# One attention and feed-forward kernel: the first batch's q and k rows laid nine to a partition, and the order of the work drawn up anew

## The chip, the core and the metric

The kernel runs on one core of a Trainium2 chip. The metric is the device time of one execution in microseconds (us), median of several runs. Beside it stands one profiled execution, from which every row below is read.

## The reference

The inputs q, k and v have 8 batches, 8 heads, 576 rows and 64 columns. Two attentions are added, and their sum goes through a gated feed-forward layer:

```python
S, D, factor = 576, 64, 4
q_d = q.reshape(B, H, S // 4, 4, D).mean(axis=3)       # k_d and v_d alike
out_d = softmax(scale * q_d @ k_d.T) @ v_d              # 144 x 144 scores
out_up = np.repeat(out_d, 4, axis=2)
mask = np.abs(pos[:, None] - pos[None, :]) < 4
out_local = softmax(np.where(mask, scale * q @ k.T, -1e9)) @ v
x = (out_up + out_local).transpose(0, 2, 1, 3).reshape(4608, 512)
h = x @ w_in                                            # 512 -> 2048
g = h * np.clip(h + 3.0, 0.0, 6.0) / 6.0
out = g @ w_out                                         # 2048 -> 512
```

## The kernel before

A batch has 8 heads, taken in pairs; a pair of one batch is a **unit**, so batch 0 has the units U0 to U3, and a head of a unit fills 64 of the 128 partitions. For each unit q and k are needed turned, with the 64 columns on the partitions. Then come the pooled attention (sums of four rows in `pool4`, L428 to L434; scores L528; softmax; product with v L711) and the banded one (scores L740 in tiles of 64 columns under a mask that L732 adds; row maxima L584, subtraction L587, exponential L590 and L595, scaling L610 and L612; turning L765; product with v L783). L788 adds the two into `first`, the rows of x for that unit.

The feed-forward part is computed with every operand split into a rounded part (hi, a CAST on L128 for ACT or L130 for DVE) and the remainder (lo, L972), three matmuls for one product. The weights are split as well, in pieces `rawp0`, `rawp1`, ...: for one piece ACT does L195 and L208, DVE does L210 and L200, then a CAST makes hi and L220 makes lo. GEMM1 is L1064 (h = x w_in), then relu on ACT L1070, gate on DVE L1074, splits, and GEMM2 L1114. Four units are the four quarters of the contracted dimension of GEMM1: its matmuls with the quarter of U3 can start only when U3's `first` is split, and before that only 18 matmuls (those of U0 to U2 for two tiles of h) stand ahead of them on PE.

Everything is recorded first as a list of operations. A planner then gives each operation a due time and places them one after the other on the engines, by estimated costs (`COST`), by penalties that steer an operation to one of the engines that can do it (`PEN`, by kind of work: "lo" is L220, "xlo" L972, "ev" the copies out of PSUM, "norm" and "normd" L612, L610), and by an offset of each unit's due time (`SHIFT`, one number for a unit, 32 in all). The outcome is a fixed order of instructions on every engine; the times in the planner do not exist on the chip, which only waits for semaphores.

In batch 0 alone q and k are turned by PE. `plan_first` loads rows as they lie in memory; `turn_rows` (L404) turns 128 rows in one matmul with the identity; `evict_rows` copies the result out of PSUM (L128 on ACT, L130 on DVE) so that row p * 4 + r lands where row number p * 4 + r belongs. In the kernel before, a partition holds four consecutive rows, which covers 512 of the 576; `half` and `main` load these, and `last` loads the 64 rows left over, k's on one half of the partitions and q's on the other. So k's 512 rows, q's 512 rows and both leftovers are turned by separate groups of matmuls (4, 4 and 1), and k's turned rows need only k's load and the leftovers.

The DMAs of U0 and of the leftovers are issued by ACT and SP in turn, everything else by SP: nine issues for q and k stand on SP ahead of the first for v. Batch 1 and later load q and k turned by DMA and DVE, and the diff leaves them alone. Dummy matmuls (L1498) fill PE while it has nothing to do in the first 30 us.

Of the kernel before, what the change touches and what calls it, by code (L numbers as in the profile page):

```python
# [17 lines left out]
B, H, S, D = 8, 8, 576, 64  # L18
DM, DFF = 512, 2048
P = 128  # L20
# [11 lines left out]
ROW = 2 * D  # L32
# [24 lines left out]
def tile_local_down_attention_moe(ctx, tc, q_all, k_all, v_all, _qk_loc, _v_loc, w_in, w_out, ident_d, _mask_d, out):  # L57
# [188 lines left out]
    def src(t, first, ap):  # L246
        return bass.AP(tensor=t.tensor, offset=t.offset + first * ROW, ap=ap)
# [3 lines left out]
    def plan_first():  # L251

        def duo(d):
            if ("rows", d) not in begun:
                begun["rows", d] = buf("rawd", (0, d), [P, 2, 9, ROW])
            return begun["rows", d]

        def row0(d):
            return 2 * d * NC * RP

        def main(i, d, u, n, eng):
            t = (q_all, k_all)[i]
            if n == 1:
                eng.dma_start(duo(d)[:, u, 4 * i:4 * i + 4], src(t, row0(d) + u * S, [[4 * ROW, P], [1, 4 * ROW]]))
            else:
                eng.dma_start(
                    duo(d)[:, :, 4 * i:4 * i + 4], src(t, row0(d), [[4 * ROW, P], [S * ROW, 2], [1, 4 * ROW]]))

        def half(i, d, h, eng):
            eng.dma_start(  # L270
                duo(d)[D * h:D * h + D, 0, 4 * i:4 * i + 4],
                src((q_all, k_all)[i], row0(d) + 4 * D * h, [[4 * ROW, D], [1, 4 * ROW]]))

        def last(i, d, eng):
            eng.dma_start(
                duo(d)[i * D:(i + 1) * D, :, 8], src((q_all, k_all)[i], row0(d) + 4 * P, [[ROW, D], [S * ROW, 2], [1, ROW]]))

        def begin(eng, what, *args, size):
            o = op(eng, 0.5, partial(what, *args, {"ACT": nc.scalar, "SP": nc.sync}[eng]),
                   take=[("rawd", (0, args[1]))], size=size, dl=-1.0)  # L280
            loads.append(o)
            return o

        for d in range(2):
            for u in range(2 - d):
                for i in (1, 0):
                    n = 1 + d
                    if u + d == 0:
                        os = [begin(eng, half, i, d, h, size=dma(D, 2048)) for h, eng in enumerate(("ACT", "SP"))]
                    else:  # L290
                        os = [begin("SP", main, i, d, u, n, size=dma(n * P, 2048))]
                    for x in range(u, u + n):
                        begun["main", d, x, i] = os
                if u == 0:
                    for i in (1, 0):
                        begun["last", d, i] = begin("ACT" if i and not d else "SP", last, i, d, size=dma(2 * D, 512))

        def sums_rest():
            begun["raw rest"] = t = buf("raw4r", 0, [4 * KR, NHP, ROW])
            nc.sync.dma_start(t, src(v_all, 4 * P, [[ROW, 4 * KR], [S * ROW, NHP], [1, ROW]]))  # L300

        def raw(d):
            begun["raw", d] = t = buf("raw4", (0, d), [P, 2, 4, ROW])
            nc.sync.dma_start(t, src(v_all, row0(d), [[4 * ROW, P], [S * ROW, 2], [1, 4 * ROW]]))

        def sum_rest():
            begun["ps rest"] = ps = bank("s", ("v4", 0))
            nc.tensor.matmul(
                ps[:KR, :NHP * ROW], four[:4 * KR, :KR], begun["raw rest"].rearrange("p n e -> p (n e)"), start=True, stop=True)

        def evict_rest(eng):
            begun["rest"] = t = buf("vr0", 0, [KR, NHP, ROW])
            copy_on(eng, t.rearrange("p n e -> p (n e)"), begun["ps rest"][:KR, :NHP * ROW])

        l = op("SP", 0.5, sums_rest, take=[("raw4r", 0)], size=dma(4 * KR * NHP, 512))
        loads.append(l)
        for d in range(2):
            begun["v", d] = o = op("SP", 0.5, partial(raw, d), take=[("raw4", (0, d))], size=dma(2 * P, 2048))
            loads.append(o)
        key = "s", ("v4", 0)  # L320
        a = op("PE", 0.95, sum_rest, [l, masked[1]], take=[key], free=[("raw4r", 0)], lag=LAGT, rec=2)
        begun["vr"] = op(on("ev", NHP * ROW), 0, evict_rest, [a], take=[("vr0", 0)], free=[key])
        early_users.extend([a, begun["vr"]])
# [49 lines left out]
    def plan_unit(b, d, u, row0, k0, kv, PS, masked, early_user, due):  # L373
# [32 lines left out]
        def evict_rows(i, eng):  # L406
            if "qk" not in st:
                st["qk"] = buf("qkd" + k0, un, [P, 2, S])
            if i < 2:
                copy_on(eng, st["qk"][:, i, :4 * P].rearrange("e (p r) -> e p r", r=4),  # L410
                        st["psq", i].rearrange("e (r p) -> e p r", r=4))
            else:
                copy_on(eng, st["qk"][:, :, 4 * P:], st["psq", i][:, :P].rearrange("e (i p) -> e i p", i=2))

        if b < BY_PE:
            rk, evs = ("rawd", (0, d)), {}
            for i in (1, 0, 2):
                key = PS, ("qk", un, i)
                lds = begun["main", d, u, i] if i < 2 else [begun["last", d, x] for x in range(2)]
                a = early_user(op("PE", 0.17 if i == 2 else 0.5, partial(turn_rows, i), lds + masked[:1],  # L420
                                  take=[key, ("qkd" + k0, un)], free=[rk], lag=LAGT, rec=1 if i == 2 else 4))
                evs[i] = op(on("ev", P if i == 2 else 4 * P), 0, partial(evict_rows, i), [a], free=[key])
# [13 lines left out]
        for kind, t in (("q", q_all), ("k", k_all)):  # L436
            hk = kind, un
            if b < BY_PE:
                a = turned[kind] = [evs["qk".index(kind)], evs[2]]
            else:  # L440
                l = op("SP", 2.0, partial(ldt, t, kind), loads if b == 1 else [], take=[("qk", hk)], size=dma(4 * S, 128), nd=4)
                a = turned[kind] = [op("DVE", 0.72, partial(turn, kind), [l])]
            pooled[kind] = early_user(op(
                on("pool4", 1.0), 0, partial(pool4, kind), a, take=[("p4" + k0, hk)]))
# [1131 lines left out]
PAIR0 = 6  # L1576

SHIFT = [
# [32 lines left out]
    "ob": {"ACT": (0.6, 0.0), "DVE": (0.64, 0.0)},  # L1611
}
PEN = {
    "lo": {"DVE": -73.8},
    "low": {"DVE": -9.2},
    "whi": {"DVE": -43.5},
    "ghi": {"DVE": -19.7},
    "pool4": {"POOL": 106.6},
    "ev": {"DVE": 130.1},
    "sum4": {"POOL": 26.0},  # L1620
    "norm": {"DVE": -42.6},
    "normd": {"DVE": 29.2, "ACT": 7.3},
    "minus": {"DVE": 27.2},
    "xhi": {"DVE": 47.9},
    "xlo": {"POOL": -152.3},
    "gl": {"POOL": -18.1},
    "ob": {"DVE": 37.5},
}


# [471 lines left out]
```

## Time and profile before

| | us |
|---|---|
| median of 3 runs | 896.82 |
| their range | 896.68 to 896.88 |
| profiled execution: its own time | 893.89 |
| profiled execution: span from first to last instruction | 892.1 |
| PE busy | 884.6 (99%) |
| DVE busy | 620.9 (70%) |
| ACT busy | 420.9 (47%) |
| POOL busy | 204.2 (23%) |

The profiled execution took 1.79 us beside its span, and 2.93 us less than the median of the runs that were timed without a profile. Busy times are of the whole span; the share of one stretch can be very different, and the first 35 us are.

### The profile page before, as it was taken

The page shows a single profiled execution, that of the slowest core. Times are in us where ns is not written, and L with a number is a line of the kernel's source. Part 1 is how long each engine was busy: PE and PEld are TensorE (multiplying, and loading weights), DVE is VectorE, ACT ScalarE, POOL GpSimd, SP SyncE. Part 2 cuts the span into 40 slices and gives each one's busy share as a digit, 9 for nine tenths or more (in the row PEclk, how much of TensorE's full clock was granted, in tenths as well). Part 3 has the DMA queues.
Part 4 walks back from the last instruction along what each step waited for, and adds up shares of the span by engine and source line. Part 5 has one row for each costly group of instructions (what it writes and reads, how often), then busy time and mean ns, then how long its engine had stood idle before and what let it go on. Part 6 is the DMA issues. An engine that isn't in the chain of part 4 may idle for free.

```text
span 892.1 us, 19653 instructions
## 1 busy us (share of the span) xinstructions
PE 884.6 (99%) x7060; PEld 720.5 (81%) x7060; DVE 620.9 (70%) x1182; ACT 420.9 (47%) x1432; POOL 204.2 (23%) x278
## 2 busy tenths in 40 slices
PE   8999999999999999999999999999999999999997
PEld 5777778888888888888888888888888888888886
DVE  7998886766854676667755784667666689876541
ACT  6967754544662456344532563445444154434200
POOL 5543533311422041313230130114122000000000
PEclk9999999999999999999999999999999999999999
DMA  9996643654664456635654567555642221222431
GB/s 249 303 262 196 149 121 98 118 113 100 121 148 92 92 118 142 133 60 104 135 121 80 117 125 213 110 109 112 148 97 62 53 71 48 77 66 71 144 93 49
DMA packets 316209, 107.47 MB, mean 120 GB/s; under 512 B 249552, under 2 KB 295632, under 8 KB 316112
## 3 DMA queue, kind: packets, MB, share of 16 engines
q1 hardware_dynamic: 315494, 105.44, 49.8%
q8 instruction: 56, 0.92, 0.4%
q10 hardware_dynamic: 618, 0.77, 0.3%
q14 instruction: 41, 0.34, 0.1%
HBM read 77.25 MB, written 28.90 MB: 119 GB/s over the span
## 4 chain that ended last, share of the span: by engine, by line
PE 98%; ACT 1%; DMA 0%; ACTq 0%; issue 0%
PE o L1114 35%; PE h L1064 34%; PE o L1329 5%; PE a L1265 5%; PE h L1265 4%; PE a L1329 2%; PE h L1329 2%; PE a L740 2%; PE h L783 2%; PE a L545 1%; PE h L690 1%; PE o L1064 1%; PE a L528 0%; DMA arena<-in_q_dram 0%; PE a L711 0%; PE a L783 0%
## 5 line engine op out<-in xcount | busy, mean ns | idle before, releaser
L1114 PE MATMUL o<-wp,rounded 128*128 128x512 f32 x1344 | 323.1, 393 | 0.0
L1064 PE MATMUL h<-rounded,wp 128*128 128x512 f32 x1320 | 309.4, 391 | 0.0
L1114 PEld LDWEIGHTS o<-wp,rounded 128*128 128x128 f32 x1344 | 249.4, 188 | 53.4 <-issue 0.8
L1064 PEld LDWEIGHTS h<-rounded,wp 128*128 128x128 f32 x1320 | 246.8, 188 | 52.2 <-issue 1.0
L1070 ACT ACTIVATE arena<-h 128x512 f32<-128x512 f32 x110 | 65.3, 593 | 153.8 <-PE h L1064 149.0
L1074 DVE SCALAR_TENSOR_TENSOR arena<-arena,h 128x512 f32<-128x512 f32 x110 | 74.8, 680 | 76.8 <-ACT arena L1070 76.1
L1082 POOL TENSOR_TENSOR rounded<-arena,rounded 128x512 fp32r<-128x512 f32 x38 | 51.4, 1353 | 129.2 <-PE o L1114 113.1
L595 ACT ACTIVATE taken<-taken,arena 128x64 f32<-128x64 f32 x240 | 80.1, 336 | 0.4
L1082 DVE TENSOR_TENSOR rounded<-arena,rounded 128x512 fp32r<-128x512 f32 x74 | 51.2, 692 | 35.2 <-PE o L1114 28.4
L130 DVE CAST rounded<-arena 128x512 fp32r<-128x512 f32 x95 | 40.3, 426 | 41.2 <-PE a L1329 19.4
L128 ACT CAST rounded<-arena 128x512 fp32r<-128x512 f32 (+6 forms) x63 | 38.6, 614 | 29.4 <-DVE arena L1074 15.5
L1329 PE MATMUL o<-wp,rounded 128*128 128x512 f32 x192 | 47.8, 392 | 0.0
L474 POOL TENSOR_TENSOR arena<-arena 96x256 f32<-96x256 f32 (+1 forms) x21 | 15.8, 754 | 139.0 <-DMA arena<-in_v_dram 139.0
L595 ACT ACTIVATION_READ_ACCUMULATOR taken<-taken,arena 128x1 f32 x240 | 45.3, 189 | 0.0
L396 DVE STREAM_TRANSPOSE taken<-taken 128x576 f32<-128x576 f32 x56 | 42.8, 767 | 1.6 <-DMA taken<-in_k_dram 0.8
L472 DVE TENSOR_REDUCE arena<-arena 128x128 f32<-128x512 f32 (+1 forms) x31 | 33.2, 1069 | 13.6 <-PE h L690 9.2
L1329 PEld LDWEIGHTS o<-wp,rounded 128*128 128x128 f32 x192 | 36.1, 188 | 8.0
L128 ACT COPY taken<-h 64x72 f32<-64x72 f32 x96 | 20.3, 211 | 30.1 <-PE h L699 22.2
L715 ACT ACTIVATE arena<-h 128x144 f32<-128x144 f32 x24 | 7.0, 290 | 57.7 <-PE h L699 57.5
L475 POOL TENSOR_TENSOR arena<-arena 96x128 f32<-96x128 f32 (+1 forms) x21 | 10.0, 478 | 94.7 <-PE h L699 94.2
L571 ACT ACTIVATE arena<-arena 128x1 f32<-128x1 f32 (+1 forms) x78 | 15.1, 194 | 33.4 <-DVE arena L584 33.1
L612 POOL TENSOR_TENSOR taken<-taken,arena 128x432 f32<-128x432 f32 (+1 forms) x21 | 22.6, 1075 | 30.8 <-DVE arena L605 27.7
(259 smaller groups left out, 1240.0 us busy)
## 6 DMA issues: line engine op xcount, KB each, us to landing
taken<-in_v_dram SPq DMA_DIRECT2D x58, 160.0 KB
rawp<-in_w_in_dram SPq DMA_DIRECT2D x16, 512.0 KB
rawp<-in_w_out_dram SPq DMA_DIRECT2D x16, 512.0 KB
taken<-in_q_dram SPq DMA_DIRECT2D x112, 72.0 KB
taken<-in_k_dram SPq DMA_DIRECT2D x112, 72.0 KB
pl<-taken SPq DMA_DIRECT2D x24, 320.0 KB
arena<-pl SPq DMA_DIRECT2D x96, 80.0 KB
arena<-in_v_dram SPq DMA_DIRECT2D x28, 256.0 KB
```

What stands on the lines that cost most here:

```text
L128: nc.scalar.copy(out_, in_)
L130: eng.tensor_copy(out_, in_)
L396: nc.vector.transpose(out=qk[kind], in_=qk[kind])
L472: eng.tensor_reduce(out=vd, in_=raw.rearrange("p r e -> p e r"), op=ALU.add, axis=AX.X)
L595: nc.scalar.activation(x[:, j], x[:, j], AF.Exp, bias=m[:, j:j + 1], scale=0.125, accum_out=s[:, j:j + 1])
L1064: nc.tensor.matmul(st["ps"], win[w][:, wt, kk * P:(kk + 1) * P], xs[part][:, kk], start=(kk == 0 and i == 0), stop=(kk == NK - 1 and i == ...
L1070: nc.scalar.activation(st["t"], st["ps"], AF.Relu, bias=3.0)
L1074: nc.vector.scalar_tensor_tensor(out=t, in0=t, scalar=6.0, in1=st["ps"], op0=ALU.min, op1=ALU.mult)
L1082: eng.tensor_tensor(st["gl"], st["t"], st["gh"].bitcast(F32), op=ALU.subtract)
L1114: nc.tensor.matmul(otile[n, m], gt[:, ms], wout[w][:, wt], start=(f == 0 and i == 0), stop=(f == NF - 1 and i == 2),)
L1265: nc.tensor.matmul(ps, w[:, wt, kk * P:(kk + 1) * P], x[part][:, kk], start=start and kk == 0 and i == 0, stop=stop and kk == 1 and i == 2 ...
L1329: nc.tensor.matmul(otile[n + two, m], g[:, m * P:(m + 1) * P], wout[f][:, wt], start=(f == 0 and i == 0), stop=(f == NF - 1 and i == 2), s ...
```

## The change

The 576 rows of a head pair are 64 times nine. After the change a partition holds nine consecutive rows, q on partitions 0 to 63 and k on 64 to 127. One DMA brings q of a unit and one brings k, 64 pieces of 4608 bytes each (U2 and U3 together, two such pieces to a partition); `half` and `last` are gone. k of U0 is issued by ACT, the rest by SP, so that five issues stand on SP ahead of v, and one on ACT instead of three. Each of the nine matmuls that turn a unit now takes 64 rows of q and 64 of k together (groups of 4, 4 and 1), so the first of them needs both loads, and `pool4` and the scores need all three copies out of PSUM. These copies write with a distance of nine elements (36 bytes) and read PSUM in order; before they wrote in order in groups of four elements and read PSUM with a distance of 128 elements. The counts of transposes and of these copies are the same; six more dummy matmuls stand in PE's first 30 us. Besides, the first 8 of the 32 numbers of `SHIFT` (the units of batches 0 and 1) and all values of `PEN` are other numbers.

```diff
         def main(i, d, u, n, eng):
+            to = duo(d)[i * D:(i + 1) * D]
             t = (q_all, k_all)[i]
             if n == 1:
-                eng.dma_start(duo(d)[:, u, 4 * i:4 * i + 4], src(t, row0(d) + u * S, [[4 * ROW, P], [1, 4 * ROW]]))
+                eng.dma_start(to[:, u], src(t, row0(d) + u * S, [[9 * ROW, D], [1, 9 * ROW]]))
             else:
-                eng.dma_start(
-                    duo(d)[:, :, 4 * i:4 * i + 4], src(t, row0(d), [[4 * ROW, P], [S * ROW, 2], [1, 4 * ROW]]))
-
-        def half(i, d, h, eng):
...
-        def last(i, d, eng):
...
+                eng.dma_start(to, src(t, row0(d), [[9 * ROW, D], [S * ROW, 2], [1, 9 * ROW]]))
...
+                    o = begin("ACT" if i and not u and not d else "SP", main, i, d, u, n, size=dma(n * D, 9 * ROW * 4))
                     for x in range(u, u + n):
-                        begun["main", d, x, i] = os
...
+                        begun["main", d, x, i] = o
...
+            to = st["qk"].rearrange("e i (p r) -> e r i p", r=9)
             if i < 2:
-                copy_on(eng, st["qk"][:, i, :4 * P].rearrange("e (p r) -> e p r", r=4),
-                        st["psq", i].rearrange("e (r p) -> e p r", r=4))
+                copy_on(eng, to[:, 4 * i:4 * i + 4], st["psq", i].rearrange("e (r i p) -> e r i p", r=4, i=2))
             else:
-                copy_on(eng, st["qk"][:, :, 4 * P:], st["psq", i][:, :P].rearrange("e (i p) -> e i p", i=2))
+                copy_on(eng, to[:, 8], st["psq", i][:, :P].rearrange("e (i p) -> e i p", i=2))
...
-            for i in (1, 0, 2):
+            for i in range(3):
                 key = PS, ("qk", un, i)
-                lds = begun["main", d, u, i] if i < 2 else [begun["last", d, x] for x in range(2)]
+                lds = [begun["main", d, u, x] for x in range(2)]
...
-                a = turned[kind] = [evs["qk".index(kind)], evs[2]]
+                a = turned[kind] = [evs[i] for i in range(3)]
...
 SHIFT = [
-    -91.4, -301.1, 33.8, -110.1, 13.1, -2.3, 0.7, -263.4,
+    -251.7, -361.6, 41.5, -18.4, 9.2, -46.2, -0.7, -322.1,
...
 PEN = {
-    "lo": {"DVE": -73.8},
+    "lo": {"DVE": -42.9},
...
```

The new numbers move instructions on every engine in the first part of the program; from the 324th matmul of the feed-forward part on, PE's order is the same in both. In the changed file every line behind L300 stands 15 lines earlier (L1064 is L1049, L972 is L957). Three places of the order follow; names end in a buffer's number.

On ACT this is the place around the copy of U3's pooled result (`o2_642` before, `o2_673` after, 128x144), without which U3's `first` cannot be added up. Before:

```order
L195 ACTIVATE rawp1_481<-rawp1_481 128x512
L208 ACTIVATE rawp1_481<-rawp1_481 128x512
L195 ACTIVATE a0_639<-rawp2_487 128x512
L128 COPY early_419<-o1_631 128x384
L128 COPY early_419<-a1_636 128x256
L128 CAST rounded_67<-first_507 128x288
L128 COPY early_247<-o2_642 128x144
```

And after the change:

```order
L195 ACTIVATE o3_619<-rawp2_448 128x512
L208 ACTIVATE rawp2_448<-rawp2_448 128x512
L128 CAST rounded_67<-first_495 128x288
L128 CAST rounded_67<-first_495 128x224
L195 ACTIVATE rawp5_474<-rawp5_474 128x512
L128 COPY early_408<-a0_641 128x3x2x48
L208 ACTIVATE rawp5_474<-rawp5_474 128x512
L128 COPY early_418<-o0_654 128x384
L128 COPY early_418<-o1_661 128x256
L195 ACTIVATE rawp3_477<-rawp3_477 128x512
L128 CAST wp1_678<-early_112 128x512
L128 CAST wp5_681<-early_114 128x512
L128 COPY early_201<-o2_673 128x144
```

The second step of piece 2, both steps of piece 5, the first of piece 3 and the hi of pieces 1 and 5 have come ahead of that copy; the hi of piece 0 has gone from ACT to DVE.

On DVE this is the place around the additions of U3 (L788 before, L773 after, with `o0_666`, `o1_667` before and `a0_684`, `o3_685` after). Before:

```order
L220 TENSOR_TENSOR wp1_662<-early_152,wp1_662 128x512
L788 TENSOR_TENSOR first_507<-o0_666,early_247 128x288
L788 TENSOR_TENSOR first_507<-o1_667,early_247 128x224
L200 SCALAR_TENSOR_TENSOR a0_639<-a0_639,rawp2_487 128x512
L788 TENSOR_TENSOR first_507<-o3_606,early_247 128x64
L788 TENSOR_TENSOR first_507<-o1_667,early_247 128x64
L972 TENSOR_TENSOR rounded_67<-first_507,rounded_67 128x224
```

And after the change:

```order
L220 TENSOR_TENSOR wp1_678<-early_112,wp1_678 128x512
L220 TENSOR_TENSOR wp5_681<-early_114,wp5_681 128x512
L773 TENSOR_TENSOR first_495<-a0_684,early_201 128x288
L773 TENSOR_TENSOR first_495<-o3_685,early_201 128x224
L130 CAST rounded_67<-first_495 128x288
L130 CAST rounded_67<-first_495 128x224
L957 TENSOR_TENSOR rounded_67<-first_495,rounded_67 128x288
L957 TENSOR_TENSOR rounded_67<-first_495,rounded_67 128x224
```

The lo of piece 5 now stands ahead of U3's additions, and all four splits of U3 come behind them on DVE; before, ACT made the two hi and POOL one of the two lo.

On PE this is the start of the feed-forward matmuls (L1064 before, L1049 after). Before:

```order
L711 MATMUL o2_642<-early_373,early_193 64x144 x4
L1064 MATMUL h0_651<-rounded_67,wp0_599 128x512 x6
...
L783 MATMUL o1_667<-early_419,early_216 64x61 x2
L1064 MATMUL h1_693<-rounded_67,wp1_662 128x512 x3
L1064 MATMUL h0_651<-rounded_67,wp0_599 128x512 x3
L1064 MATMUL h1_693<-rounded_67,wp1_662 128x512 x6
L1064 MATMUL h0_651<-rounded_67,wp0_599 128x512 x3
```

And after the change:

```order
L1049 MATMUL h0_623<-rounded_67,wp0_588 128x512 x6
L606 MATMUL a0_641<-ident_73,early_192 128x128 x3
...
L1049 MATMUL h0_623<-rounded_67,wp0_588 128x512 x3
L696 MATMUL o2_673<-early_408,early_192 64x144 x4
...
L768 MATMUL o3_685<-early_418,early_214 64x61 x2
L1049 MATMUL h1_709<-rounded_67,wp1_678 128x512 x9
L1049 MATMUL h0_623<-rounded_67,wp0_588 128x512 x3
```

In both the last row shown is the first that needs the quarter of U3, and 18 matmuls of this part stand ahead of it; nine of them, not six, now come ahead of U3's last product with v.

## Rows read from the trace of the kernel before

**Rows 1.** The page: busy time of each engine, and the chain that ended last.

```profile
PE 884.6 (99%) x7060; PEld 720.5 (81%) x7060; DVE 620.9 (70%) x1182; ACT 420.9 (47%) x1432; POOL 204.2 (23%) x278
...
PE 98%; ACT 1%; DMA 0%; ACTq 0%; issue 0%
```

**Rows 2.** Timeline of PE, 31 to 44 us: start, busy, what, how often.

```profile
32.98 0.81 PE L783 MATMUL o<-early 64*64 64x60 f32 x40
33.72 4.37 PE L1064 MATMUL h<-rounded,wp 128*128 128x512 f32 x18
37.93 5.89 PE L1064 MATMUL o<-rounded,wp 128*128 128x512 f32 x24
```

**Rows 3.** Timeline of DVE, 32 to 37 us.

```profile
32.52 0.42 DVE L130 CAST wp<-early 128x512 fp32r<-128x512 f32 x1
32.85 0.46 DVE L972 TENSOR_TENSOR rounded<-first,rounded 128x288 fp32r<-128x288 f32 x1
33.22 0.69 DVE L220 TENSOR_TENSOR wp<-early,wp 128x512 fp32r<-128x512 f32 x1
33.89 0.76 DVE L788 TENSOR_TENSOR first<-o,early 128x288 f32<-128x288 f32 x2
...
35.42 0.86 DVE L972 TENSOR_TENSOR rounded<-first,rounded 128x224 fp32r<-128x224 f32 x1
```

**Rows 4.** Waits of ACT in the first 40 us: total, times, longest.

```profile
ACT arena L128 <- PE o L404: 0.9, 1, 0.9
```

**Rows 5.** Timeline of the start: transposes, first scores, first maximum, ACT's last late copy.

```profile
3.98 1.08 PE L404 MATMUL a<-ident,arena 128*128 128x128 f32 x4
...
5.71 0.66 PE L404 MATMUL a<-ident,arena 128*128 128x128 f32 x4 [0.65 <-DMA arena<-in_q_dram]
6.28 0.44 PE L404 MATMUL o<-ident,arena 128*128 128x128 f32 x2
...
7.57 0.27 PE L740 MATMUL o<-taken 64*64 64x64 f32 x2
...
9.10 0.48 DVE L584 TENSOR_REDUCE arena<-o 128x5 f32<-128x320 f32 x1
...
10.48 0.58 ACT L128 COPY arena<-o 128x512 f32<-128x512 f32 x1 [0.89 <-PE o L404]
```

**Rows 6.** Timeline of ACT, 31 to 37 us.

```profile
32.52 0.26 ACT L128 COPY early<-o 128x144 f32<-128x144 f32 x1
32.69 0.37 ACT L128 CAST rounded<-first 128x224 fp32r<-128x224 f32 x1
32.97 1.26 ACT L195 ACTIVATE rawp<-rawp 128x512 f32<-128x512 f32 x2
34.12 0.64 ACT L208 ACTIVATE rawp<-rawp 128x512 int32<-128x512 uint32 x1
34.67 0.70 ACT L128 CAST rounded<-first 128x288 fp32r<-128x288 f32 x2
35.34 0.59 ACT L128 CAST wp<-a 128x512 fp32r<-128x512 f32 x1
35.82 1.14 ACT L195 ACTIVATE rawp<-rawp 128x1024 f32<-128x1024 f32 x1
```

**Rows 7.** Windows: engines' busy time and instructions, clock, DMA share, GB/s.

```profile
0.00:5.00 5.00, 3.33 (x9) 1.30 (x9) 0.80 (x5) 1.49 (x2) 1.77 (x12) 1.00 0.48 141
5.00:10.00 5.00, 4.36 (x72) 3.30 (x72) 4.01 (x9) 1.17 (x2) 1.92 (x4) 1.00 1.01 328
```

**Rows 8.** Groups by line and form, first 36 us: count, busy us, mean ns.

```profile
L610 ACT ACTIVATE early<-early,arena 128x144 f32<-128x144 f32 x3 | 1.0, 413 | 0.0
...
L475 POOL TENSOR_TENSOR early<-early 128x128 f32<-128x128 f32 x3 | 1.4, 455 | 0.2
...
L432 POOL TENSOR_TENSOR early<-taken 128x144 f32<-128x144 f32 x1 | 0.4, 446 | 0.8 <-ACT taken L128 0.8
```

**Rows 9.** Timeline of POOL, 33 to 37 us.

```profile
35.23 0.81 POOL L972 TENSOR_TENSOR rounded<-first,rounded 128x288 fp32r<-128x288 f32 x1 [0.42 <-ACT rounded L128]
```

More of the change, by code (lines that the diff above doesn't have):

```diff
@@ L261, in main @@
         def main(i, d, u, n, eng):
+            to = duo(d)[i * D:(i + 1) * D]
             t = (q_all, k_all)[i]
             if n == 1:
-                eng.dma_start(duo(d)[:, u, 4 * i:4 * i + 4], src(t, row0(d) + u * S, [[4 * ROW, P], [1, 4 * ROW]]))
+                eng.dma_start(to[:, u], src(t, row0(d) + u * S, [[9 * ROW, D], [1, 9 * ROW]]))
             else:
-                eng.dma_start(
-                    duo(d)[:, :, 4 * i:4 * i + 4], src(t, row0(d), [[4 * ROW, P], [S * ROW, 2], [1, 4 * ROW]]))
-        def half(i, d, h, eng):
-            eng.dma_start(
-                duo(d)[D * h:D * h + D, 0, 4 * i:4 * i + 4],
-                src((q_all, k_all)[i], row0(d) + 4 * D * h, [[4 * ROW, D], [1, 4 * ROW]]))
-        def last(i, d, eng):
-            eng.dma_start(
-                duo(d)[i * D:(i + 1) * D, :, 8], src((q_all, k_all)[i], row0(d) + 4 * P, [[ROW, D], [S * ROW, 2], [1, ROW]]))
+                eng.dma_start(to, src(t, row0(d), [[9 * ROW, D], [S * ROW, 2], [1, 9 * ROW]]))
         def begin(eng, what, *args, size):
@@ L287, in plan_first @@
                     n = 1 + d
[L288 to L291, printed above, removed]
+                    o = begin("ACT" if i and not u and not d else "SP", main, i, d, u, n, size=dma(n * D, 9 * ROW * 4))
                     for x in range(u, u + n):
-                        begun["main", d, x, i] = os
-                if u == 0:
-                    for i in (1, 0):
-                        begun["last", d, i] = begin("ACT" if i and not d else "SP", last, i, d, size=dma(2 * D, 512))
+                        begun["main", d, x, i] = o
         def sums_rest():
@@ L1613 @@
 PEN = {
-    "lo": {"DVE": -73.8},
[L1615 to L1627, printed above, removed]
+    "lo": {"DVE": -42.9},
+    "low": {"DVE": 41.4},
+    "whi": {"DVE": -11.0},
+    "ghi": {"DVE": 83.1},
+    "pool4": {"POOL": 88.7},
+    "ev": {"DVE": 116.4},
+    "sum4": {"POOL": -22.5},
+    "norm": {"DVE": -61.1},
+    "normd": {"DVE": 59.2, "ACT": 36.5},
+    "minus": {"DVE": 45.7},
+    "xhi": {"DVE": 10.1},
+    "xlo": {"POOL": -122.6},
+    "gl": {"POOL": 45.9},
+    "ob": {"DVE": 46.9},
 }
```

## Prediction, made before the changed kernel was run

> **What bounds the kernel now.** I read the page first. PE is busy for 99% of the span and the chain that ended last is PE for 98% [rows 1], so almost nothing but PE's own work and its holes can change the time. The feed-forward matmuls cannot be shortened here: the change leaves their count alone, and 24 of them run from 37.93 us, in 5.89 us by their modelled end. The 18 before them begin at 33.72 and the next begin at 37.93 [rows 2], so one takes at most (37.93 - 33.72) / 18 = 0.234 us; I use 0.23. From 33.72 us on PE therefore goes without a hole worth naming, and the order of the matmuls is the same in both kernels from the 324th on. What is left to win or lose is the moment at which this unbroken run begins.
>
> So I read the timelines backwards from there. Of the 18 matmuls, 12 need only U0 to U2 and the next three need the split rows of U3, so U3's quarter is wanted at 33.72 + 12 x 0.23 = 36.5 us. The last remainder of U3 is made on DVE from 35.42 for 0.86 us, that is until 36.28 [rows 3]. PE and the splitting of U3 meet within 0.2 us. Any delay of the last remainder of U3 beyond that is a hole in PE, one for one, since after it nothing in the 850 us behind can give it back.
>
> Who makes U3 late or early? ACT's last wait before 40 us that costs anything in this stretch is 0.9 us [rows 4], and it ends at 10.48 us [rows 5]; from there ACT has work without a break until U3's pooled result is copied at 32.52 [rows 6]. An engine that is full from 10.5 to 32.5 us is a sum: what the new order puts ahead of the copy delays it, and what begins sooner brings it forward. This is the place to count.
>
> **The start.** Before, PE turns k from 3.98, waits for q until 5.71 and turns the last rows from 6.28 to 6.72; scores follow at 7.57, that is 0.85 later, and the first maximum on DVE at 9.10, behind the pooling of U1 [rows 5]. After, all nine matmuls need both loads. The first 5 us moved 141 GB/s x 5 us = 705 KB, the next run at 328 GB/s [rows 7]. q and k of U0 are 2 x 64 x 4608 B = 590 KB and now come first, so I put their landing (705 - 590) / 328 = 0.35 us ahead of 5.00, at about 4.65. Four transposes took 1.08 us at 3.98 and 0.66 at 5.71 [rows 5]; nine take about 4 x 0.27 + 5 x 0.15 = 1.8 us, until 6.45. That is 0.3 us sooner than 6.72, and the scores come at about 7.3. The maxima can follow 0.8 us later, since in the new order only a copy of U1, not its pooling, stands between: 8.1 against 9.10. The gain handed on to ACT is thus between **0.3 and 1.0 us**. That k's half-loads used to arrive first was worth little, because scores waited for the last rows anyway; the two issues fewer on ACT and four fewer on SP ahead of v lie in time in which the 16 DMA engines are full (share 1.01 [rows 7]), and I cost them at nothing beyond this.
>
> **ACT ahead of U3's copy.** Compared as counts by form up to that copy, the new order has more: two steps L195 and two L208 of 512 columns, one cast of 512, one L610 group of three, one copy of 144; and less: one copy of 512. A copy of 288 columns stands in place of a cast of 288. From start to start, two L195 took 34.12 - 32.97 = 1.15 us, an L208 34.67 - 34.12 = 0.55, a cast of 512 35.82 - 35.34 = 0.48, the copy of 144 columns 0.17 [rows 6]. An L610 is 0.413 us [rows 8] less the 0.09 by which neighbours overlap (32.78 - 32.69 [rows 6]), three of them 0.96; the copy of 512 is 0.58 less 0.09 [rows 5]. Sum: 1.15 + 1.10 + 0.48 + 0.96 + 0.17 - 0.49 = **3.4 us**. The copy of U3's pooled result begins at 32.52 + 3.4 less 0.3 to 1.0, at 34.9 to 35.6.
>
> **DVE behind it.** In the new order the cast that makes hi of weight piece 5 ends about 0.1 us after that copy begins (35.0 to 35.7), its lo on DVE takes 0.67 (33.22 to 33.89) and stands ahead of U3's additions. So these begin at 35.7 to 36.4, and not before. Then: additions 0.76 - 0.09 = 0.67; two casts, which ACT used to make, together 512 columns, at 0.33 for one of 512 (32.52 to 32.85) and a little for the second, 0.36; the remainder of 288 columns 0.37 (32.85 to 33.22); that of 224 columns between 0.29 (by its columns) and 0.78 (the row at 35.42, which ran beside POOL), taken as 0.5 [rows 3]. Sum 1.9. The last remainder of U3 ends at **37.6 to 38.3** against 36.28. What passes between a remainder's end and PE's start is not shown apart; before it is 0.2 us or less (36.28 to 36.5), so the run of PE is late by 1.1 to 2.0 us, **1.6** in the middle. PE itself would be there earlier: U3's last product with v took 0.81 us [rows 2] and needs the copies that end some 1.5 us (one L195, two casts) ahead of the pooled copy, so by about 35.0; nine matmuls more make 37.1. PE would then stand for the difference.
>
> DVE's own sum does not decide. Counted by form like ACT's, its work up to the additions grows by about 1.8 us (two L200 and two L220 more, a normalisation, a pooling and two remainders fewer, and small ones), an estimate from the same views; 33.89 + 1.8 - 0.3 = 35.4, ahead of the 35.7 that ACT allows.
>
> **What is moved later.** Piece 5's parts are finished earlier than before, so DVE and ACT have that much less to do behind U3. But PE had no hole there [rows 2], so this buys nothing. All six remainders of U0 to U2 go to POOL, and so do U3's two normalisations, behind four of them. If U3's turning has to wait there for one remainder of 288 columns, that is up to 0.81 us [rows 9] more on ACT; below it costs nothing. This bound sets the top of the likeliest range: 2.0 + 0.7 = 2.7. The bottom is 1.1 - 0.2 = 0.9, with the remainder of 224 columns at 0.29.
>
> The six dummy matmuls more stand where PE waits in the first 30 us, before the run that counts, and cost nothing as long as ACT decides when U3's last product begins (by 35.0 against the 37.6 that is waited for).
>
> **The copies out of PSUM.** They now write every ninth element. No row of before shows such a write by ACT or DVE. Nearest is POOL's sum that reads every fourth element: 446 ns for 144 columns, 3.1 ns each, against 455 ns for 128 in a row, 3.6 each [rows 8]. By these a distance costs nothing, and I take nothing. The upper bound is a doubling of each, 0.5 us, with two of ACT's four copies of 512 columns ahead of the full stretch and two in it: 1.0 us more. [...]
>
> **Rivals and chances.** The profiled run of before is 893.89 us, its median without a profile 896.82; all shifts go onto the median. What this kernel's measurement can tell from no change I take as 0.2%, 1.8 us.
>
> - *The forecast*, the new order makes U3's split late by 0.9 to 2.7 us: 897.7 to 899.5, middle **898.4**. Chance 0.58, split by the bound (1.8, in the upper half of it) into 0.30 within and 0.28 above.
> - *The start gives it back.* With a gain g at the start, U3's split ends at 32.52 + 3.4 + 0.1 + 0.67 + 1.9 - g = 38.6 - g. At g = 1.5, half as much again as the maxima show, that is 37.1, and the shift 0.6 to 0.8; at 2.3 it is none: 896.8 to 897.7. For it speaks that ACT is a pure sum; against it that U1 to U3 load behind full DMA engines. Chance 0.16, all within 0.2%.
> - *Writing at a distance costs*, or a second wait on POOL adds up: beyond 2.7, 899.5 to 901. Against it POOL's row; chance 0.07, slower.
> - *Faster.* One mechanism: ACT's full stretch begins much sooner. Its last late copy is at 10.48 and its own work is hardly 1.8 us before that [rows 5], so up to 4 us of waiting are there to be had, if both rows of U0 and U1 land near 3.8 us (590 KB at 328 GB/s is 1.8 us) and the transposes run at 0.15 us each throughout. It decides from a gain g: above 2.3 it is faster than before, above 4.1 by 0.2%, and at 4.5 the time is 896.8 - 2.2 = 894.6. Against it the rate of 141 GB/s in the first 5 us. Chance 0.19, of which 0.15 beyond 0.2%, since an error of mine in ACT's sum would show as this too.
>
> Faster 0.15, within 0.2% 0.30 + 0.16 + 0.04 = 0.50, slower 0.28 + 0.07 = 0.35. The range must leave out no more than 2 in 10. It cuts half of the slow rival at 900.3 and most of the fast one at 895.2.
>
> **What would show it.** In the profile after: transposes in one piece from about 4.7; scores at 7.1 to 7.4; the first maximum near 8.1; ACT without waits from about 10; the copy of U3's pooled result at 34.9 to 35.6; the last L957 of U3 on DVE ending at 37.6 to 38.3, with a wait of PE for DVE of about 1 us just there; from the 324th matmul on the same pace; span 892.1 + 1.6 = 893.7. Wrong would be: a copy out of PSUM that takes over 0.9 us, ACT with holes between 12 and 33 us (then slower than I say), or U3's pooled copy before 33.5 (then not slower at all).

## The result, and the profile after

The changed kernel took 903.48 us (median of 4 runs, 901.51 to 904.72) against 896.75 (896.6 to 896.88): a ratio of 1.008, 95% interval 1.0066 to 1.0094, that is 6.7 us slower, outside the range of the prediction. The profiled execution of after took 904.72 us with a span of 902.5. Later runs timed the kernel before between 894.49 and 897.85 us, so its profiled execution (893.89) is a quick one, and a difference read between the two traces (10.8 us) is some 4 us larger than that of the medians (6.7).

The windows of the profile after (columns as in [rows 7]):

```profile
0.00:5.00 5.00, 3.17 (x7) 0.89 (x7) 0.80 (x5) 1.49 (x2) 1.77 (x12) 1.00 0.58 135
5.00:10.00 5.00, 2.53 (x21) 1.81 (x25) 2.31 (x4) 1.06 (x1) 1.18 (x3) 1.00 1.03 219
...
15.00:20.00 5.00, 4.65 (x20) 2.62 (x21) 1.67 (x6) 1.62 (x5) 3.30 (x6) 0.54 1.15 295
20.00:25.00 5.00, 5.00 (x70) 4.17 (x68) 4.26 (x8) 4.92 (x15) 2.51 (x4) 0.77 1.17 245
```

From 5 to 10 us the DMA engines are as full as before (1.03 against 1.01), and yet move 219 GB/s where they moved 328. In this pair of windows a full engine was no measure of what it moved. Behind that, ACT and DVE are idle for most of 15 to 20 us (busy for 1.62 and 1.67 us), and the granted clock falls to 0.54 and 0.77 in these windows, with 0.50 in each us from 16 to 22; the PE groups there are few (20 matmuls from 15 to 20 us).

PE's waits of 0.4 us and more (total, times, longest):

```profile
PE o L293 <- DMA early<-in_v_dram: 1.7, 1, 1.7
PE h L1483 <- DVE identb L147: 1.7, 1, 1.7
PE a L389 <- DMA arena<-in_k_dram: 1.5, 1, 1.5
PE o L389 <- DMA arena<-in_q_dram: 1.1, 1, 1.1
PE o L1099 <- DVE arena L1008: 0.4, 1, 0.4
```

The start of PE's timeline:

```profile
6.36 1.06 PE L389 MATMUL a<-ident,arena 128*128 128x128 f32 x8 [1.53 <-DMA arena<-in_k_dram]
7.26 0.27 PE L389 MATMUL o<-ident,arena 128*128 128x128 f32 x1
7.37 0.59 PE L1483 MATMUL h<-identb 128*128 128x512 bf16 x2
9.07 0.63 PE L389 MATMUL o<-ident,arena 128*128 128x128 f32 x4 [1.11 <-DMA arena<-in_q_dram]
9.54 0.43 PE L717 MATMUL o<-maskb,identb 128*128 128x320 bf16 x2
9.90 0.29 PE L725 MATMUL o<-taken 64*64 64x64 f32 x4
```

U0's transposes begin at 6.36, where 4.65 was forecast, and U1's at 9.07. The first scores stand behind U1's first four transposes in PE's order and come at 9.90 against 7.57 [rows 5], and the sum of v's left-over rows (L293) waits for v, which stands behind q and k in the same queue. The end of the stretch in ACT's timeline:

```profile
43.45 0.27 ACT L128 COPY early<-o 128x144 f32<-128x144 f32 x1
```

In DVE's:

```profile
45.37 0.74 DVE L957 TENSOR_TENSOR rounded<-first,rounded 128x288 fp32r<-128x288 f32 x2
```

And in PE's:

```profile
46.17 1.43 PE L1049 MATMUL h<-rounded,wp 128*128 128x512 f32 x5 [0.17 <-DVE rounded L957]
```

U3's pooled copy begins at 43.45 (32.52 before [rows 6]), the last remainder ends at 46.11 (36.28 [rows 3]) and PE goes on at 46.17. It stood idle for only 0.17 us there, where about 1 us was forecast: its own work came almost as late as the remainder. The lines behind have no wait of PE above 0.4 us: the 9.8 us between the two remainders are, within 0.6, the 10.4 between the two spans.

### The profile page after: what moved, and what is told of

It reads as the page before. It is cut to its first block, busy times and chain, and to the rows that moved or that the text cites. A ratio compares the mean times of both kernels' runs of the same rounds, so it can differ in the third digit from the quotient of the medians.

```text
span 902.5 us, 19674 instructions
## 1 busy us (share of the span) xinstructions
PE 890.4 (99%) x7066; PEld 722.7 (80%) x7066; DVE 617.4 (68%) x1165; ACT 435.7 (48%) x1451; POOL 198.4 (22%) x277
## 4 chain that ended last, share of the span: by engine, by line
PE 94%; DMA 2%; SPq 2%; DVE 1%; ACT 1%; issue 0%; POOL 0%; DVEq 0%; POOLq 0%
PE o L1099 34%; PE h L1049 32%; PE o L1314 5%; PE a L1250 5%; PE h L1250 4%; PE a L1314 2%; PE h L1314 2%; PE a L725 2%; PE h L768 2%; DMA early<-in_v_dram 1%; PE a L530 1%; PE h L675 1%; DMA rawp<-in_w_in_dram 1%; SPq L375 1%; PE a L696 0%; PE a L768 0%
## 5 line engine op out<-in xcount | busy, mean ns | idle before, releaser
L1049 PE MATMUL h<-rounded,wp 128*128 128x512 f32 x1332 | 313.2, 391 | 0.5 <-POOL rounded L957 0.3
L1049 PEld LDWEIGHTS h<-rounded,wp 128*128 128x128 f32 x1332 | 248.8, 188 | 54.2 <-issue 0.8
L1067 DVE TENSOR_TENSOR rounded<-arena,rounded 128x512 fp32r<-128x512 f32 x84 | 60.4, 719 | 65.6 <-PE o L1099 58.7
L128 ACT CAST rounded<-arena 128x512 fp32r<-128x512 f32 (+5 forms) x88 | 53.6, 614 | 66.1 <-PE o L1099 44.7
L1067 POOL TENSOR_TENSOR rounded<-arena,rounded 128x512 fp32r<-128x512 f32 x28 | 36.4, 1300 | 127.5 <-PE o L1099 117.8
L130 DVE CAST rounded<-arena 128x512 fp32r<-128x512 f32 (+2 forms) x70 | 30.1, 432 | 22.2 <-PE a L1314 19.5
L413 DVE TENSOR_REDUCE arena<-taken 128x144 f32<-128x576 f32 x39 | 28.4, 744 | 2.1 <-PE a L513 1.4
```

The source lines that it names most:

```text
L128: nc.scalar.copy(out_, in_)
L130: eng.tensor_copy(out_, in_)
L1049: nc.tensor.matmul(st["ps"], win[w][:, wt, kk * P:(kk + 1) * P], xs[part][:, kk], start=(kk == 0 and i == 0), stop=(kk == NK - 1 and i == ...
L1067: eng.tensor_tensor(st["gl"], st["t"], st["gh"].bitcast(F32), op=ALU.subtract)
```

## Experiments

Each group of runs was timed beside its own runs of the kernel before, whose median moved between 895.46 and 896.75. Times of one group compare directly; across groups, "over before" is the fairer measure. By it the changed kernel is 6.7 us over.

The first four ran together, beside a median of 895.46 for before. Their question was which part of the layout is slow.

**Loads cut in two.** The same 64 partitions, shorter pieces:

```diff
-            if n == 1:
-                eng.dma_start(to[:, u], src(t, row0(d) + u * S, [[9 * ROW, D], [1, 9 * ROW]]))
...
+            for r, m in ((0, 4), (4, 5)):
+                if n == 1:
+                    eng.dma_start(to[:, u, r:r + m], src(t, row0(d) + u * S + r, [[9 * ROW, D], [1, m * ROW]]))
...
```

> The changed kernel, with each load of nine rows a partition cut into two, of four rows (2048 bytes a piece) and of five (2560 bytes); still 64 partitions at a time. Theory A (half the partitions take only half the rate): GB/s from 5 to 10 us stays at 210 to 240, the first transposes at 6.3 us or later, time 902 to 905. Rival B (pieces of 4608 bytes are too long): the rate rises above 320 GB/s, first transposes by 5.2 us, time 898.5 to 901.

903.28 us, 7.8 over before (ratio 1.0083, 95% interval 1.0061 to 1.0105). The window from 5 to 10 us:

```profile
5.00:10.00 5.00, 3.59 (x58) 2.37 (x57) 2.96 (x4) 1.07 (x1) 1.24 (x3) 1.00 1.07 221
```

221 GB/s with pieces of 2048 and 2560 bytes: the size of the pieces is not it. The time of the first transposes was missed, since the first half of a unit's rows now lands alone and four of them run at 4.62; the next four wait until 6.69.

**k on a queue of its own.**

```diff
-                    o = begin("ACT" if i and not u and not d else "SP", main, i, d, u, n, size=dma(n * D, 9 * ROW * 4))
+                    o = begin("ACT" if i else "SP", main, i, d, u, n, size=dma(n * D, 9 * ROW * 4))
```

> The changed kernel, with all of k issued by ACT (three issues) and all of q by SP, so that loads into the two halves of the partitions stand on two queues side by side; sizes as in the change. Theory A: both halves fill at once, 320 to 400 GB/s from 4 us on, second unit's transposes by 7 us against 9.07, no clock drop at 15 us, time 898.5 to 901. Rival B: the rate stays at 210 to 240 GB/s, second unit as late as before, time 902.5 to 904.5.

900.49 us, 5.0 over before (1.0053, 1.0035 to 1.0071). That is 3.0 less than the changed kernel by the times and 1.7 less by the difference over before, and the two intervals overlap a little. Its windows:

```profile
5.00:10.00 5.00, 3.73 (x16) 3.12 (x17) 2.10 (x3) 1.08 (x1) 0.45 (x2) 1.00 1.03 251
...
15.00:20.00 5.00, 4.62 (x70) 3.62 (x73) 5.00 (x13) 4.92 (x18) 4.69 (x9) 1.00 1.22 228
```

The time and the clock are as theory A has them. The rate is not: 251 GB/s is above 219, far from 320. The first unit comes no earlier (6.27 us), and U1's first transposes are again at 9.07, here without a wait for their rows. PE itself was slow before them:

```profile
6.27 1.94 PE L389 MATMUL a<-ident,arena 128*128 128x128 f32 x8 [1.44 <-DMA arena<-in_k_dram]
```

Eight transposes took 1.94 us against 1.06 in the changed kernel, although the window gives the granted clock as 1.00; why, no run here shows. What is gained lies behind: from 10 to 15 us this run moves 308 GB/s against 204, and v is no longer waited for at L293.

**Copies in groups of four.**

```diff
-                copy_on(eng, to[:, 4 * i:4 * i + 4], st["psq", i].rearrange("e (r i p) -> e r i p", r=4, i=2))
+                copy_on(eng, to[:, 4 * i:4 * i + 4].rearrange("e r i p -> e i p r"),
+                        st["psq", i].rearrange("e (r i p) -> e i p r", r=4, i=2))
```

> The changed kernel, with the copies of four rows out of PSUM walked the other way: four neighbouring elements written at a time, PSUM read at a distance, as in the kernel before; the same rows in the same places. Theory C (writing every ninth element doubles a copy): copies of 512 columns fall from 1.07 to 0.58 (ACT) and 0.69 us (DVE), each unit's scores 0.4 us sooner, time 901.5 to 903 while loads stay slow. Rival D (the copies are long because the engines share something else with the slow loads): they stay above 0.95 us, time 903 to 904.

902.92 us, 7.5 over before (1.0082, 1.0062 to 1.0102). Groups by line and form, first 30 us, of the changed kernel:

```profile
L128 ACT COPY taken<-a 128x512 f32<-128x512 f32 x2 | 2.1, 1071 | 7.4 <-PE a L389 7.4
...
L130 DVE COPY taken<-o 128x512 f32<-128x512 f32 x1 | 1.1, 1095 | 0.4 <-PE o L389 0.4
```

And of this one:

```profile
L128 ACT COPY taken<-a 128x512 f32<-128x512 f32 x2 | 1.3, 658 | 7.4 <-PE a L389 7.4
...
L130 DVE COPY taken<-o 128x512 f32<-128x512 f32 x1 | 0.7, 692 | 0.7 <-PE o L389 0.7
```

The copies follow theory C. ACT's groups of four, which start 36 bytes apart, keep 0.08 us over the 0.58 of before. The time moves by no more than noise (0.6 us less than the changed kernel by the times, 0.7 more by the difference over before): while loads are late, a shorter copy buys little.

**Both.**

> Both edits at once: k on ACT's queue, copies in groups of four. What is left against the kernel before is the new order alone. If the prediction's sum for the order holds (1.6 us, 0.9 to 2.7): 897.7 to 899.5. If the order costs nothing and loads and copies were all: 896.0 to 897.5. If the order is the larger part of the 6.7 us lost: above 900.

899.92 us, 4.5 over before (1.0044, 1.0027 to 1.0062): above the range for the order's cost alone, and 0.6 below the run with k on ACT's queue. The first scores are still at 10.26, so this run doesn't yet isolate the order.

The next three ran beside a median of 896.14.

**The new order alone.** The plan is that of the changed kernel; only what its steps carry out is as before:

```diff
-            to = st["qk"].rearrange("e i (p r) -> e r i p", r=9)
             if i < 2:
-                copy_on(eng, to[:, 4 * i:4 * i + 4], st["psq", i].rearrange("e (r i p) -> e r i p", r=4, i=2))
+                copy_on(eng, st["qk"][:, i, :4 * P].rearrange("e (p r) -> e p r", r=4),
+                        st["psq", i].rearrange("e (r p) -> e p r", r=4))
...
```

and the loads likewise. Two things are still not those of before: U0's rows come in one load each instead of two half-loads, with the leftover rows issued right behind, and all transposes of a unit wait for both loads. What these cost is counted with the order here.

> The order of every engine as in the changed kernel, row for row, but loads, transposes and copies out of PSUM in the layout of the kernel before (four rows to a partition on all 128, the 64 rows left over apart). It measures the new order alone. The prediction's sum for the order: 1.6 us over before (0.9 to 2.7), U3's last remainder at 37.6 to 38.3. Rival, the order is what is left in the run with both edits: 3.5 us or more over before, with holes on ACT between 10 and 33 us. Rival, loads and copies were all: within 0.9 us of before.

898.89 us, 2.75 over before (1.0032, 1.0019 to 1.0045, or 1.7 to 4.0 us). Between the first two theories by the median: more than the 1.6 of the sum and just beyond its range, less than 3.5; the interval reaches into both. ACT's timeline at the end of the stretch:

```profile
37.95 0.27 ACT L128 COPY early<-o 128x144 f32<-128x144 f32 x1
```

DVE's:

```profile
39.86 0.74 DVE L958 TENSOR_TENSOR rounded<-first,rounded 128x288 fp32r<-128x288 f32 x2
```

The largest waits of ACT between 5 and 45 us, but for those on the first transposes:

```profile
ACT wp L128 <- DVE early L200: 1.0, 1, 1.0
ACT early L128 <- PE o L294: 0.8, 1, 0.8
ACT early L557 <- DVE early L570: 0.6, 1, 0.6
```

The pooled copy begins at 37.95 and the last remainder ends at 40.60, where the expectation had 37.6 to 38.3. The first scores are at 8.22, 0.65 later than before instead of sooner. The windows up to the pooled copy (columns as in [rows 7]), before and here:

```profile
0.00:32.52 32.52, 29.82 (x465) 20.41 (x466) 26.56 (x69) 24.28 (x80) 19.55 (x37) 1.00 0.98 297
0.00:37.95 37.95, 34.20 (x516) 22.82 (x517) 30.01 (x73) 28.30 (x88) 22.00 (x41) 1.00 0.91 257
```

ACT is busy for 28.30 us instead of 24.28, 4.0 more. For the rest of the time it is idle: 9.65 us instead of 8.24, 1.4 more. And PE is hardly ahead of the remainder:

```profile
37.79 2.70 PE L1050 MATMUL h<-rounded,wp 128*128 128x512 f32 x10
40.66 1.43 PE L1050 MATMUL h<-rounded,wp 128*128 128x512 f32 x5 [0.17 <-DVE rounded L958]
```

Its unbroken run begins with these ten matmuls at 37.79, behind U3's last product with v, and it is idle for 0.17 us only.

**All partitions.** q of two units in one DMA, k of two in another, both over 128 partitions (for U0 and U1 each is cut into rows 0 to 3 of a partition and rows 4 to 8); each transpose then takes 64 partitions:

```diff
+            r, m = (0, 9) if d else ((0, 4), (4, 5))[u]
+            eng.dma_start(duo(d)[:, i, r:r + m], src((q_all, k_all)[i], row0(d) + r, [[9 * ROW, P], [1, m * ROW]]))
...
+                for x in range(2):
+                    nc.tensor.transpose(
+                        out=ps[:, n * P + x * D:n * P + x * D + D], in_=begun["rows", d][u * D:u * D + D, x, 4 * i + n],
+                        identity=ident[u * D:u * D + D, u * D:u * D + D])
```

> Order and nine rows to a partition as in the changed kernel, but each load fills all 128 partitions (q of two units in one piece of memory, k of two in the other; rows 0 to 3 of a partition first, then 4 to 8), transposes take 64 partitions at a time, and the copies write groups of four. Theory A (half the partitions take half the rate): 320 GB/s or more from 3 us on, last first-unit transpose by 6.5 us, time within 0.8 us of the run with the new order alone. If pieces of nine rows cost something else too: 1.5 us or more above that run.

903.14 us, 7.0 over before (1.0082, 1.0068 to 1.0096): the rate as theory A has it, the time not at all, and the first unit's last transpose at 7.43 instead of 6.5. Its windows:

```profile
5.00:10.00 5.00, 3.80 (x50) 2.62 (x54) 2.43 (x4) 0.66 (x1) 1.42 (x3) 0.89 1.04 351
10.00:15.00 5.00, 5.00 (x67) 3.56 (x62) 2.93 (x7) 2.02 (x6) 2.10 (x5) 0.50 1.13 294
```

351 GB/s at the same fullness of the engines (1.04). But PE waited twice for rows (0.6 and 0.7 us), and from 10 to 15 us the granted clock was 0.50.

**The kernel before, writing at a distance of 16 bytes.**

```diff
-                copy_on(eng, st["qk"][:, i, :4 * P].rearrange("e (p r) -> e p r", r=4),
-                        st["psq", i].rearrange("e (r p) -> e p r", r=4))
+                copy_on(eng, st["qk"][:, i, :4 * P].rearrange("e (p r) -> e r p", r=4),
+                        st["psq", i].rearrange("e (r p) -> e r p", r=4))
```

> The kernel before, with its copies out of PSUM walked the other way: PSUM read in order, every fourth element written (16 bytes apart), the same values in the same places. Theory C (a write that goes to another 16 bytes each time doubles the copy): copies of 512 columns at 1.0 us or more on ACT and DVE against 0.58 and 0.69, time 0.4 to 2 us above before. Rival: only a distance beyond 16 bytes costs, copies and time as before.

897.12 us, 1.0 over before (1.0013, 1.0004 to 1.0022). Its groups by line and form, first 30 us:

```profile
L128 ACT COPY arena<-o 128x512 f32<-128x512 f32 x2 | 2.2, 1093 | 1.0 <-PE o L404 1.0
...
L130 DVE COPY taken<-o 128x512 f32<-128x512 f32 x1 | 1.1, 1090 | 0.0
```

Theory C again, in the layout and order of before: the distance of the write does it, on both engines, and 16 bytes are enough (1.09 us on each). (PSUM is read in order here, which by itself cost nothing: the cast of 512 columns from PSUM in [rows 6] reads in order and took 0.59.)

The next three ran beside a median of 896.48.

**Piece 5 behind U3.**

```diff
+        at = max(order.index(o) for o in self.mark) + 1
+        moved = [o for o in order[:at] if o in self.late]
+        order[:at] = [o for o in order[:at] if o not in moved] + moved
```

(`mark` holds the splits of the first tile, `late` the five operations.)

> The run with the new order alone, with one thing put back: the five operations of weight piece 5 (two steps and the hi on ACT, one step and the lo on DVE) stand behind U3's splits instead of ahead of them. Theory E (what ACT and DVE have to do ahead of U3's pooled copy and additions sets the start of the unbroken run): the pooled copy moves from 37.95 us to about 36.4, U3's last remainder from 40.6 to 38.6 to 39.2, time 1.2 to 2.0 us below the run with the new order alone, that is 0.7 to 1.5 over before. Rival F (the late start of the first units sets it, the added work fits into holes): pooled copy moves by less than 0.5 us, time as in the run with the new order alone, 2.3 to 3.2 over before.

900.86 us, 4.4 over before (1.0047, 1.0034 to 1.006): 1.6 slower than the new order alone by the difference over before, though the intervals overlap, and in no case the gain expected. ACT's timeline:

```profile
36.83 0.27 ACT L128 COPY early<-o 128x144 f32<-128x144 f32 x1
```

DVE's:

```profile
38.63 0.75 DVE L960 TENSOR_TENSOR rounded<-first,rounded 128x288 fp32r<-128x288 f32 x2
```

The largest wait of PE behind the start:

```profile
PE h L1054 <- DVE arena L1064: 1.7, 1, 1.7
```

The pooled copy and the last remainder came 1.1 and 1.2 us sooner, somewhat less than expected, so theory E holds in kind for them. But pieces 5 and 3 and the gate then meet on ACT and DVE, ACT and DVE wait for each other's halves of a piece, and PE waits 1.7 us for a gate at 43.7 us. What the new order does early has a use that my sum didn't give it.

**More dummy matmuls**, in the changed kernel and in the one that loads into all partitions (a count by name of the step):

```diff
+            o.busy = (o.busy or 0) + {('turn_rows', 1): 4, ('turn_rows', 4): 3, ('sum_rest', 1): 9}.get((name, seen[name]), 0)
```

> The changed kernel, with 16 dummy matmuls more on PE where it stood waiting for loads (4 ahead of the first transposes, 3 ahead of U1's, 9 ahead of the sum of v's rows left over). Theory G (the fall of the granted clock to 0.54 and 0.77 from 15 to 25 us follows from these waits and is on the path): clock 1.00 in all windows from 10 us on, U2's transposes at 0.66 us for four instead of 1.1, time 900.5 to 902.5. Rival H (PE is not on the path there, the loads and ACT's and DVE's work are): clock 1.00, time 902.7 to 904.5.

903.16 us, 6.7 over before like the changed kernel (1.0073, 1.0059 to 1.0086), with the clock at 1.00 in every window:

```profile
15.00:20.00 5.00, 5.00 (x39) 2.94 (x36) 3.08 (x9) 3.14 (x10) 3.20 (x6) 1.00 1.15 290
20.00:25.00 5.00, 4.63 (x110) 3.15 (x109) 5.00 (x12) 4.60 (x17) 4.08 (x7) 1.00 1.17 254
```

Rival H: the clock alone was not what held the changed kernel back.

> The run that loads nine rows a partition into all 128 partitions, with 7 dummy matmuls more on PE ahead of transposes that waited. Theory G (its clock of 0.50 from 10 to 15 us made it as slow as the changed kernel): clock 1.00 in all windows, time 899 to 900.5, near the run with the new order alone. Rival (its finer transposes and the wait for two units' rows cost the same without the clock): 902 to 904.

899.49 us, 3.0 over before (1.0036, 1.0022 to 1.0049), 3.65 below the same kernel without them by the times and 4.0 by the difference over before (2, 3 and 2 dummies ahead of three groups of transposes). Its windows:

```profile
5.00:10.00 5.00, 5.00 (x57) 2.81 (x59) 2.44 (x4) 0.66 (x1) 1.38 (x3) 1.00 1.04 352
10.00:15.00 5.00, 5.00 (x112) 3.36 (x103) 4.58 (x12) 3.63 (x13) 2.80 (x6) 1.00 1.13 292
```

Here the loss went with the clock: same rate, same order, 112 matmuls from 10 to 15 us instead of 67. Nine rows to a partition, loaded into all partitions and copied in groups of four, cost no more than the new order alone (3.0 over before here, 2.75 there).

**The sum of v's left-over rows later**, beside a median of 895.77 for before:

```diff
...
+        moved = [o for o in order if name(o) in ("sum_rest", "evict_rest")]
+        order = [o for o in order if o not in moved]
+        at = [k for k, o in enumerate(order) if name(o) == "turn_rows"][7] + 1
+        order[at:at] = moved
...
```

> The run with the new order alone, with one step put back a little: the sum of v's rows left over (PE, two matmuls, which waited 1.0 us for v) and its copy on ACT (which waited 0.8 us) stand behind the pooled scores of U1 and the first transposes of U2, not ahead. Theory I (the order puts a wait for a late load ahead of work that is ready, on PE and on ACT, and ACT's sum carries it on): these waits vanish, U3's pooled copy at 37.0 to 37.4 instead of 37.95, time 0.5 to 1.0 us below the run with the new order alone, 1.7 to 2.3 over before. Rival J (ACT would have waited for DVE next anyway): pooled copy at 37.8 or later, time unchanged within 0.3 us.

898.92 us, 3.15 over before (1.0035, 1.0022 to 1.0048), no gain over the new order alone: rival J. The trace, of an execution of 901.24 us, 2.3 above that median, has the pooled copy at 38.64. PE's wait for v is gone, but PE now waits for ACT, and ACT's wait of 0.8 us for the sum is still there, in the waits of PE and of ACT:

```profile
PE o L390 <- ACT early L128: 0.7, 1, 0.7
...
ACT early L128 <- PE o L294: 0.8, 1, 0.8
```

> The changed kernel with the same step put back: the sum of v's rows left over and its copy behind U1's pooled scores and U2's first transposes. Theory I: PE no longer waits 1.7 us for v at 15 us, DVE no longer 2.8 us for U1's pooled scores, the clock does not fall so far, time 901 to 902.3. Rival J: the rows of U2 and v land late in any case and the next steps wait for them, time 902.7 to 904.

902.5 us, 6.7 over before like the changed kernel (1.0072, 1.0058 to 1.0086); the time itself lies between the two ranges. The clock stayed at 1.00 and DVE's wait of 2.8 us for U1's pooled scores is gone, without a gain that can be told from nothing. No version that beats the kernel before came out of these runs.

## Why the prediction was wrong

**What bounds the kernel: right in the main.** The loss is the time at which PE's unbroken run with U3's quarter begins; behind it PE has no wait above 0.4 us in the traces of both kernels. The step from U3's pooled copy to the last remainder was sized well: 0.1 + 0.67 + 1.9 = 2.7 us forecast, 46.11 - 43.45 = 2.66 after the change, 40.60 - 37.95 = 2.65 with the order alone. But "PE itself would be there earlier" failed. It was to stand for 0.5 to 1.2 us and stood for 0.17, in both runs, since its own work ahead was nearly as late. A sooner remainder alone would have won little.

**The start: the step that failed.** U0's rows "now come first, so I put their landing (705 - 590) / 328 = 0.35 us ahead of 5.00, at about 4.65". This took the rates of [rows 7] over for loads into half of the partitions, took U0 to move alone, and costed the loads of U1 and behind at nothing. By 5.00 us 135 x 5 = 675 KB had moved, more than U0's 590, so rows of others were among them, and from 5 to 10 us the rate was 219 with the engines full (1.03). U0's transposes began at 6.36, U1's, which stand ahead of the first scores, at 9.07, and v came behind them. In place of a gain of 0.3 to 1.0 us the first scores came 2.3 us late.

Loads into 64 partitions, one after another, moved 219 to 221 GB/s from 5 to 10 us, whether a piece has 4608 bytes or about 2048 (loads cut in two); as soon as a DMA spans all partitions the same window has 351. So half of the partitions had 0.62 of that rate; why, no run here shows. This fits U1 and what follows. It is not the whole of U0's lateness: U0's two loads fill both halves from two queues after the change as well, as the half-loads did before. In the first 5 us 135 GB/s were moved, against 184 in the run with the new order alone, and k's other loads on ACT's queue didn't make U0 earlier (6.27). What else held U0 was not taken apart.

**The copies out of PSUM: a rival that came true.** I took nothing, by a row of POOL that reads every fourth element. ACT's and DVE's writes are another matter: 0.58 and 0.69 us became 1.05 to 1.11 at 36 bytes and 1.07 to 1.09 at 16. That is about the doubling of the upper bound, which was an estimate of mine that no row of before showed. It is also the mechanism of the rival that got a chance of 0.07, though its time (899.5 to 901) wasn't met either. A copy over 0.9 us and ACT with holes (2.3 us up to 17.20) were two of the prediction's own signs of being wrong, and both were seen. The row I set against a cost of the distance is of POOL, and of a read: it spoke neither of the engines in question nor of writes. The share of the long copies in the time is about 1 us where it stands alone (1.0 in the kernel before, interval 0.4 to 2.0), and not to be told from noise beside late loads.

**The order: right place, size off.** 1.6 us forecast, 2.75 measured by the medians; 1.6 lies just outside the interval of 1.7 to 4.0. In the trace, on whose rows the sum was built, U3's last remainder was 4.3 us late (40.60 against 36.28), not 1.3 to 2.0. The trace of before is of an execution 2.3 us below its median, though, and where these 2.3 us lie no run shows. Two terms were off. ACT's added work is 4.0 us (28.30 - 24.28), not 3.4. And the start, put down as a gain of 0.3 to 1.0, was a loss: ACT is idle for 1.4 us more, with new waits of 0.8 us for the sum of v's rows and 0.6 for DVE, for which I had only a bound by POOL. Taking one wait of this kind away (PE's for v) brought another in its place. And "this buys nothing" was wrong of piece 5: moved behind U3, it made PE wait 1.7 us.

**The clock** was in no part of the prediction. In the changed kernel bringing it back to 1.00 gained nothing clear (0.3 us by the times); with loads at 351 GB/s it was worth 3.65 us.

Together: the order is 2.75 us (with the two things counted in that its section names), which leaves 4.0 of the 6.7 for the layout. No single part of these 4.0 shows alone. Copies in groups (7.5 over before), the clock (6.7) and loads over all partitions with copies in groups (7.0) each left the time where it was; loads over all partitions, copies in groups and the clock together brought it to 3.0, all but 0.3. k on a second queue, which also kept the clock, gave back 1.7 to 3.0. It looks as if late loads and the low clock each hide what curing the other gains. How the 4.0 divide between late rows of U1 to U3, late v and the copies was not taken apart.

## What to carry to other kernels

Before counting on a load to land sooner, ask which partitions it writes: DMA engines at a share of 1.03 moved 219 GB/s into one half at a time, and at 1.04 351 into both. Let the write of a copy run over neighbouring elements (0.58 us on ACT, where every fourth or ninth took 1.05 to 1.09) and put the distance on the side of PSUM, which cost ACT nothing here (0.58 us, as a cast of 512 columns read in order, 0.59 [rows 6]). Where loads are late and the clock is low, cure both before judging either: here neither alone changed the time (7.0 and 6.7 us over before), and both together, with copies in groups, left 3.0. That the planner's order fits only the landing times it was made for is a guess; what the runs show is that putting single steps of it later gained nothing in three runs.

## What the runs showed of the hardware that was not expected

- The share of busy DMA engines said nothing of the rate: 1.01 at 328 GB/s, 1.03 at 219, 1.04 at 351, all from 5 to 10 us.
- A copy of 512 columns from PSUM took 1.05 to 1.11 us on ACT and DVE when it wrote every fourth or ninth element, and 0.58 (ACT) and 0.69 (DVE) when it read every 128th and wrote in groups of four in a row.
- Two waits of 0.6 and 0.7 us for rows, between 4.8 and 6.9 us, were followed by a granted clock of 0.50 from 10 to 15 us; seven dummy matmuls more ahead of the transposes kept it at 1.00.
- With all of k on ACT's queue and q on SP's, 251 GB/s were moved from 5 to 10 us and 308 from 10 to 15, where the changed kernel, with only U0's k on ACT's, moved 219 and 204.
